# Spectral mixing and a routed mixture of experts: result tiles of 96 rows made into tiles of 128 rows

## The chip, the cores and the metric

The kernel runs on one core of one Trainium2 chip. The metric is the device time of one execution in microseconds. The engines are called as the profile calls them: PE is TensorE (PEld its weight loads), DVE is VectorE, ACT is ScalarE, POOL is GpSimd, SP is SyncE, which here only issues DMAs. A "q" behind a name (SPq, POOLq) is that engine's instruction queue.

## The reference, cut to what matters

```python
# x: (8, 2496, 256) float32; N = 8 * 2496 = 19968 rows; E = 8 experts; F = 1024
X = np.fft.rfft(x, axis=1)
y = np.fft.irfft(X * (filt_r + 1j * filt_i)[None], n=2496, axis=1)     # mixing along the sequence
x = y.reshape(19968, 256)
logits = x @ w_gate + modality_bias[modality_id]                       # 8 logits a row
e_idx = argmax(logits);  gate_w = softmax(logits)[e_idx]
for e in range(8):                                                     # top-1 experts
    mask = e_idx == e
    out[mask] = gate_w[mask, None] * (np.maximum(x[mask] @ w1[e], 0) @ w2[e])
```

## The kernel before, in words

**Transforms.** The length 2496 is split as 48 x 52, and both FFTs are done as small matrix products in three stages per batch. Stage 1 (`stage1`) multiplies 26 tiles of 96 rows by a fixed 96 x 96 matrix and stores the result to DRAM (`b1_d`). Stage 2 (`stage2`) reads it back transposed, multiplies 24 slices of 104 rows, applies the filter and multiplies again, and stores to `b2_d`. Stage 3 (`stage3`) reads `b2_d` back as 26 tiles of 96 rows (`t4`, four DMA loads for tiles 0-7, 8-15, 16-23 and 24-25), multiplies each by the matrix `wbm` (96 x 96, L433) into a PSUM tile `ps`, and evicts two tiles at a time (EV = 2) into `yo`: row `p`, tile `t` is sequence position `26 p + t`. The evictions go to ACT (L451) and DVE (L453) in turn. One step later the two tiles are transposed on PE (L441), copied to SBUF as `yT` (L443), multiplied by the gate weights (L446), and the eight logits of each row are added to `lg` (L456).

**Routing.** When all 26 tiles of a batch are through, `route` finds each row's expert and gate weight and its position in that expert's bin, by DVE operations on tiles of [96, 26, 8] and two small matmuls (L463 to L496). `table` then works out which blocks of 256 rows are full in which bin. `scatter` sends every tile's 96 rows (256 fp16 values, the row number and the gate weight, 520 bytes) to its bin in DRAM with one indirect DMA from POOL (L501), 26 for a batch.

**Experts.** A block is 256 rows of one expert. `load` reads it from its bin (L575, from SP, buffer `xs`, five of them). `turn` copies the expert's w1 (L588), copies row numbers and gate weights out of `xs` into `meta` (L594, three buffers), transposes the rows (L598, L599). `up` (L609) and `down` (L622) run in four quarter steps q of 4 + 4 matmuls of 256 columns, with a ReLU eviction on ACT (L614) between them. After the last quarter DVE multiplies by the gate weights into `osb` (L629, two buffers), and two indirect DMAs from POOL write 128 rows each to the output (L632). These two read `osb` for the data and `meta` for the row numbers, so both buffers are held until the DMA has landed.

**Order.** The main loop below runs 12 iterations `i` of 14 steps `k`. In one iteration stage 1 works on batch i, stage 2 on batch i-1, stage 3 on batch i-2, and the scatters on batch i-3, two of each a step. Each step ends with three quarter steps of the expert work. `route` and `table` for batch i-2 come at the end of an iteration. The number of blocks that are certain to be full by then is fixed (1, 10, 10, 10, 9, 10, 10, and 25 for the last batch, 85 in all), so after the last scatters some 25 blocks remain, which run with nothing beside them. The framework orders the instructions of each engine at build time; on the chip every engine works through its list in that order and waits where it must. A scatter is kept behind the last issued output DMA (`behind("out", 1)`). A block's load waits for all scatters that precede it in the program.

Of the kernel before, what the change touches and what calls it, by code (L numbers as in the profile page):

```python
# [20 lines left out]
P = 128  # L21
# [7 lines left out]
def kernel(  # L29
# [30 lines left out]
    KB = 2 * N2  # L60

# [238 lines left out]
    keep = const_pool.tile([KA, E, NTT], F32)  # L300
# [27 lines left out]

    mid_h = dataclasses.replace(moe_modality_id.tensor, shape=list(moe_modality_id.tensor.shape))
    mid32 = mid_h.ap().bitcast(I32).rearrange("(n two) -> n two", two=2)  # L330
# [18 lines left out]
    NP = NTT // EV  # L349
    st = [dict() for _ in range(B)]  # L350
# [57 lines left out]
    def stage3(g, k):  # L408

        t = k * EV  # L410
        if k == 0:
            yw = yp.tile([KA, NTT, RW], I32, tag="yo", name="yo")
# [3 lines left out]
            nc.sync.dma_start(mid_raw, mid32[g * S:(g + 1) * S].rearrange("(p t) two -> p t two", t=NTT))  # L416
            midf = sp.tile([KA, NTT], F32, tag="midf")
            nc.vector.tensor_copy(midf, mid_raw[:, :, 0])
            lg = sp.tile([KA, NTT, E], F32, tag="lg", bufs=2)
            st[g]["lg"] = lg  # L420
            nc.vector.tensor_mul(lg, midf[:, :, None].to_broadcast([KA, NTT, E]),
                                 biasd[:KA, None, :].to_broadcast([KA, NTT, E]))
            nc.vector.tensor_add(lg, lg, bias0[:KA, None, :].to_broadcast([KA, NTT, E]))
        yo = st[g]["yw"].bitcast(BF16)
        if k < NP:
            c, t0, t1 = chunk_of(t)
            if t == t0:
                src = b2_d[g].rearrange("s (jr t) c -> (s jr) t c", jr=4)
                st[g]["t4"] = bp.tile([KA, TCM, D], BF16, tag="t24", name="t4")
                nc.sync.dma_start(st[g]["t4"][:, 0:t1 - t0, :], src[:, t0:t1, :])  # L430
            ps = pp.tile([P, EV, D], F32, tag="ps")
            for i in range(EV):
                nc.tensor.matmul(ps[:KA, i, :], lhsT=wbm, rhs=st[g]["t4"][:, t - t0 + i, :], start=True, stop=True)  # L433
        if k > 0:
            tb = t - EV
            lt = pp.tile([P, 2 * D], F32, tag="ps")
            pT = lt[:, 0:D].bitcast(BF16).rearrange("p (i a q) -> p i a q", i=EV, a=DC)
            psL = lt[:, D:D + EV * E].rearrange("p (i e) -> p i e", e=E)
            for i in range(EV):
                for dc in range(DC):  # L440
                    nc.tensor.transpose(pT[:, i, dc, :KA], yo[:, tb + i, dc * P:(dc + 1) * P], ident[:KA, :KA])  # L441
            yT = sp.tile([P, EV, DC, KA], BF16, tag="yT", bufs=2)
            nc.vector.tensor_copy(yT, pT[:, :, :, :KA])  # L443
            for i in range(EV):
                for dc in range(DC):
                    nc.tensor.matmul(psL[:KA, i, :], lhsT=yT[:, i, dc, :], rhs=wg[:, dc, :],  # L446
                                     start=(dc == 0), stop=(dc == DC - 1))
        if k < NP:
            dst = yo[:, t:t + EV, 0:D]
            if k % 2:  # L450
                nc.scalar.activation(dst, ps[:KA], AF.Copy, scale=1.0 / S)  # L451
            else:
                nc.vector.tensor_scalar_mul(dst, ps[:KA], 1.0 / S)  # L453
        if k > 0:
            lg = st[g]["lg"]
            nc.vector.tensor_add(lg[:, tb:tb + EV], lg[:, tb:tb + EV], psL[:KA])  # L456

    def route(g):

        yw, lg = st[g]["yw"], st[g]["lg"]  # L460
        b3 = [KA, NTT, E]
        mx = sp.tile([KA, NTT], F32, tag="mx")
        nc.vector.reduce_max(mx, lg, axis=AX.X)  # L463
        oh = sp.tile(b3, F32, tag="oh")
        nc.vector.tensor_tensor(oh, lg, mx[:, :, None].to_broadcast(b3), op=ALU.is_ge)
        nc.vector.tensor_mul(oh, oh, revio[:KA, None, :].to_broadcast(b3))
        wm = sp.tile([KA, NTT], F32, tag="wm")
        nc.vector.reduce_max(wm, oh, axis=AX.X)
        ohT = sp.tile([KA, E, NTT], F32, tag="ohT")
        nc.vector.tensor_tensor(ohT.rearrange("p e t -> p t e"), oh, wm[:, :, None].to_broadcast(b3),  # L470
                                op=ALU.is_equal)
        sc = sp.tile([KA, E, NTT], F32, tag="sc")
        nc.vector.tensor_tensor_scan(sc.rearrange("p e t -> p (e t)"), keep.rearrange("p e t -> p (e t)"),
                                     ohT.rearrange("p e t -> p (e t)"), 0.0, op0=ALU.mult, op1=ALU.add)
        c = sp.tile([KA, E], F32, tag="c")
        nc.vector.tensor_copy(c, sc[:, :, NTT - 1])
        psO = pp.tile([P, 2, E], F32, tag="ps")
        nc.tensor.matmul(psO[:KA, 0, :], lhsT=Lexcl[:KA, :KA], rhs=c, start=True, stop=True)
        nc.tensor.matmul(psO[:, 1, :], lhsT=ones_sq[:KA, :], rhs=c, start=True, stop=True)
        off = sp.tile([KA, E], F32, tag="off")  # L480
        nc.vector.tensor_add(off, cnt[:KA], ecap[:KA])
        nc.vector.tensor_add(off, off, psO[:KA, 0, :])
        nc.vector.tensor_add(cnt, cnt, psO[:, 1, :])
        nc.vector.tensor_add(sc, sc, off[:, :, None].to_broadcast([KA, E, NTT]))
        nc.vector.tensor_mul(sc, sc, ohT)
        pos = sp.tile([KA, NTT], F32, tag="pos")
        nc.vector.reduce_sum(pos, sc.rearrange("p e t -> p t e"), axis=AX.X)
        pos_i = sp.tile([KA, NTT], I32, tag="posi", bufs=2)
# [5 lines left out]
        ssum = sp.tile([KA, NTT], F32, tag="ssum")  # L494
        nc.vector.reduce_sum(ssum, lg, axis=AX.X)
        nc.vector.reciprocal(yw[:, :, DW + 1].bitcast(F32), ssum)  # L496

    def scatter(g, k):
        for t in range(k * EV, (k + 1) * EV):
            with behind("out", 1):  # L500
                ins = nc.gpsimd.indirect_dma_start(  # L501
                    out=bins_d[:, :], out_offset=IOA(ap=st[g]["pos"][:, t:t + 1], axis=0),
                    in_=st[g]["yw"][:, t, :], in_offset=None)
# [76 lines left out]
    def turn(b):  # L580
# [12 lines left out]
        b["meta"] = ep.tile([P, NI, 2], I32, tag="meta", bufs=3, name="meta")  # L593
# [22 lines left out]
    def down(b, q):  # L616
# [8 lines left out]
        if (q + 1) * FQ == FT:  # L625
            osb = ep.tile([P, NI, D], F32, tag="osb", bufs=2)
# [71 lines left out]
    for i in range(B + 4):  # L698
        for k in range(NP + 1):
# [6 lines left out]
            if 0 <= i - 2 < B:  # L706
                stage3(i - 2, k)
            if 0 <= i - 3 < B and k < NP:
# [44 lines left out]
```

## Time and profile before

| | |
|---|---|
| median of 3 runs | 1031.1 us (1027.1 to 1033.96) |
| profiled execution | 1031.97 us, span 1030.2 us (first to last instruction) |
| mean granted TensorE clock | 0.868 |
| PE / DVE / ACT / POOL busy | 662.1 / 424.8 / 387.0 / 409.0 us |
| scatters L501 / output DMAs L632 | 208 / 170 instructions |

The profile is one execution. A row of the groups view gives line, engine and operation, out<-in, count, busy time and mean duration, then the engine's idle time just ahead of these instructions and what ended it. The waits view gives who waited for what: total us, times, longest. The chain view follows the last instruction back through what released it; "another core or an unknown queue", shown as "remote" in the waits, is a release that the profile can't assign. In the timeline the square brackets hold the idle time before and its releaser. The windows view gives busy time of each engine in a stretch of the span. By these, set-up lasts to about 43 us, transforms alone run to about 171 us, scatters begin at 176.9 us and end near 866 us, and the last stretch, from about 870 us, is expert work only.

### The profile page before, as it was taken

Reading aid. Unit: us, or ns where it says so; the run is one execution under the profiler, and the core shown is the slowest. Engines: PE = TensorE matmul, PEld = TensorE weight load, DVE = VectorE, ACT = ScalarE, POOL = GpSimd, SP = SyncE. Lnnn points to the kernel's source line nnn. Section 1 sums busy time; section 2 is a strip of 40 time slices with the busy share of each in tenths; the row PEclk is TensorE's granted clock in tenths of the full one; section 3 lists DMA queues with packets and bytes.
Section 4 is the critical chain, followed back from the end, with each engine's and each line's share of the span. In section 5 each row is a group of like instructions: output and inputs, shape, how many; then the busy total and the mean of one; then the engine's idle time right before and its main releaser. Section 6 shows DMA issues by size and latency. Waiting matters only on the chain.

```text
span 1030.2 us, 16235 instructions
## 1 busy us (share of the span) xinstructions
PE 662.1 (64%) x4966; PEld 526.6 (51%) x4966; DVE 424.8 (41%) x1305; ACT 387.0 (38%) x697; POOL 409.0 (40%) x468
## 2 busy tenths in 40 slices
PE   0316377266645777687677776774777567768776
PEld 0205266255434666566565555563555445656554
DVE  8803145135325344633454463445335322333332
ACT  1115255143433455344444443441333233434333
POOL 6022201712442355435535543544355455333333
PEclk9999999999655898589979986896868787999999
DMA  9299965335436445534553344324111422212210
GB/s 146 36 207 208 219 147 127 91 91 129 108 87 140 115 120 116 129 99 126 123 146 92 96 120 111 91 62 113 58 57 54 118 68 78 73 62 67 68 42 2
DMA packets 95179, 106.66 MB, mean 104 GB/s; under 512 B 13226, under 2 KB 77520, under 8 KB 94994
## 3 DMA queue, kind: packets, MB, share of 16 engines
q0 software_dynamic: 32544, 52.04, 23.0%
q1 hardware_dynamic: 62554, 53.59, 20.1%
q8 instruction: 45, 0.74, 0.3%
q14 instruction: 36, 0.29, 0.1%
HBM read 74.27 MB, written 54.31 MB: 125 GB/s over the span
## 4 chain that ended last, share of the span: by engine, by line
PE 30%; issue 22%; DMA 13%; DVE 12%; another core or an unknown queue 10%; POOL 7%; ACT 4%; DVEq 1%; POOLq 0%; ACTq 0%; SPq 0%
PE hps L609 7%; PE ops L622 7%; DMA t<-b_d 5%; POOL out_dram L632 4%; DMA b_d<-t 4%; POOL bins_d L501 3%; DMA b_d<-z 2%; PE ps L433 2%; PE pz L389 2%; PE lt L446 2%; PE ps L363 2%; PE pz L390 2%; PE ps L382 2%; DVE osb L629 2%
## 5 line engine op out<-in xcount | busy, mean ns | idle before, releaser
L614 ACT ACTIVATE hT<-hps 128x512 f16<-128x512 f32 x340 | 197.0, 597 | 305.0 <-PE hps L609 164.3
L632 POOL DMA_INDIRECT out_dram<-osb,meta x170 | 166.8, 981 | 308.8 <-DVE osb L629 267.2
L622 PE MATMUL ops<-w2sb,hT 128*128 x1360 | 227.6, 291 | 46.8 <-DVE osb L629 46.3
L501 POOL DMA_INDIRECT bins_d<-yo,pos_i x208 | 193.7, 931 | 110.5 <-issue 69.7
L609 PE MATMUL hps<-xT,w 128*128 128x256 f16 x1360 | 222.2, 297 | 23.0 <-ACT hT L614 10.9
L622 PEld LDWEIGHTS <-hT 128*128 128x128 f16 x1360 | 140.6, 105 | 88.6 <-issue 57.7
L609 PEld LDWEIGHTS <-w 128*128 128x128 f16 x1360 | 138.9, 106 | 50.1 <-issue 18.2
L366 ACT CAST t<-ps 96x512 f16<-96x512 f32 x104 | 59.8, 583 | 127.7 <-PE ps L363 73.1
L599 DVE COPY xT<-pT 128x512 f16<-128x512 f16 x85 | 36.0, 424 | 146.4 <-PE pT L598 83.3
L403 ACT CAST z<-pz 104x512 f16<-104x512 f32 x96 | 56.7, 590 | 84.5 <-remote 30.7
L130 POOL DMA_DIRECT2D xt<-in_x_dram x32 | 18.2, 570 | 169.6 <-PE ps L363 158.8
L396 DVE TENSOR_TENSOR p<-xf,g 104x512 f16<-104x512 f16 x96 | 40.3, 420 | 109.1 <-ACT xf L394 94.4
L382 PE MATMUL ps<-t,w2m 104*104 104x256 f16 x192 | 52.8, 369 | 49.3 <-DMA t<-b_d 40.5
L389 PE MATMUL pz<-p,a1m 104*104 104x256 f16 x192 | 68.1, 364 | 21.0 <-issue 6.6
L433 PE MATMUL ps<-t,wbm 96*96 96x256 f16 x208 | 56.1, 354 | 37.4 <-DMA t<-b_d 15.2
L629 DVE TENSOR_SCALAR osb<-ops,meta 128x256 f32<-128x256 f32 x170 | 74.3, 476 | 9.3 <-PE ops L622 5.5
L363 PE MATMUL ps<-xt,w1m 96*96 96x256 f16 x208 | 59.0, 380 | 24.4 <-ACT z L403 8.5
L394 ACT CAST xf<-ps 104x512 f16<-104x512 f32 x96 | 56.3, 588 | 48.1 <-PE ps L382 34.2
L446 PEld LDWEIGHTS <-yT 128*96 128x96 f16 x416 | 40.9, 162 | 63.0 <-DVE yT L443 43.7
L446 PE MATMUL lt<-wg,yT 128*96 128x8 f16 x416 | 41.8, 207 | 47.2 <-DVE yT L443 32.7
L588 DVE COPY w<-w1sb 128x2048 f16 x85 | 58.8, 692 | 23.7 <-PE hps L609 18.1
L390 PE MATMUL pz<-xf,a2m 104*104 104x256 f16 x192 | 68.2, 365 | 0.0
(179 smaller groups left out, 687.3 us busy)
## 6 DMA issues: line engine op xcount, KB each, us to landing
xs<-bins_d SPq DMA_DIRECT2D x85, 130.0 KB
t<-b_d SPq DMA_DIRECT2D x24, 416.0 KB
b_d<-z SPq DMA_DIRECT2D x48, 208.0 KB
xt<-in_x_dram POOLq DMA_DIRECT2D x24, 384.0 KB
b_d<-t SPq DMA_DIRECT2D x48, 192.0 KB
t<-b_d SPq DMA_DIRECT2D x24, 384.0 KB
w1sb<-in_moe_w_dram POOLq DMA_DIRECT2D x8, 512.0 KB
w2sb<-in_moe_w_dram POOLq DMA_DIRECT2D x8, 512.0 KB
```

Of the source, the lines that this page charges most:

```text
L363: nc.tensor.matmul(ps[:KA, i, :], lhsT=w1m, rhs=xt[:, t - t0 + i, :], start=True, stop=True)
L382: nc.tensor.matmul(ps[:KB, i, :], lhsT=w2m[:, s + i, :], rhs=st[g]["t2"][:, s % SCH + i, :], start=True, stop=True)
L389: nc.tensor.matmul(pz[:KB, i, :], lhsT=a1m[:, s_ + i, :], rhs=p1[:, i, :], start=True, stop=False)
L390: nc.tensor.matmul(pz[:KB, i, :], lhsT=a2m[:, s_ + i, :], rhs=p2[:, i, :], start=False, stop=True)
L433: nc.tensor.matmul(ps[:KA, i, :], lhsT=wbm, rhs=st[g]["t4"][:, t - t0 + i, :], start=True, stop=True)
L446: nc.tensor.matmul(psL[:KA, i, :], lhsT=yT[:, i, dc, :], rhs=wg[:, dc, :], start=(dc == 0), stop=(dc == DC - 1))
L501: ins = nc.gpsimd.indirect_dma_start(out=bins_d[:, :], out_offset=IOA(ap=st[g]["pos"][:, t:t + 1], axis=0), in_=st[g]["yw"][:, t, :], in_o ...
L609: mm = nc.tensor.matmul(hps[:, k, :], lhsT=b["w1"][:, dc, ft * P:(ft + 1) * P], rhs=b["xT"][:, dc].rearrange("p i t -> p (i t)"), start=(d ...
L614: nc.scalar.activation(b["hT"][:, q * FQ:(q + 1) * FQ, :], hps, AF.Relu)
L622: nc.tensor.matmul(b["ops"][:, i, :], lhsT=b["hT"][:, ft, i * P:(i + 1) * P], rhs=w2sb[:, ds(b["ej"], 1), ft, :], start=(ft == 0 and i == ...
L629: nc.vector.tensor_scalar_mul(osb[:, i, :], b["ops"][:, i, :], gate[:, i, :])
L632: ins = nc.gpsimd.indirect_dma_start(out=out[:, :], out_offset=IOA(ap=b["meta"][:, i, 0:1], axis=0), in_=osb[:, i, :], in_offset=None, **kw)
```

## The change

PSUM and SBUF have 128 partitions; stage 3 used 96. The 26 tiles of a batch become 20: of every four tiles (0-3, 4-7, ..., 20-23) three stay, and the fourth one's 96 rows are computed in three pieces of 32 rows into partitions 96 to 127 of the other three, by a second matmul with 32 columns of `wbm`. Tiles 24 and 25 stay at 96 rows, and their partitions 96 to 127 hold copies that are masked out. So `yo`, `lg` and everything in `route` are [128, 20, ...]; stage 3 ends at step 10 of an iteration, not 13, and there are 20 scatters a batch (18 of 128 rows, 2 of 96). Row numbers come from a table `tok` made once; POOL adds the batch's offset to it. The modality numbers of all batches are loaded and rearranged once in the set-up (`mids`), by four DMAs and seven small DVE copies, instead of per batch. The `t4` loads are issued at steps 0, 3, 6 and 9 (before: 0, 4, 8, 12). Beside this, `meta` gets 8 buffers instead of 3 and `osb` 3 instead of 2.

```diff
+    KC = P - KA                       # 32
+    NYF = NTT // 4 * 3                # 18
+    NY = NYF + 2                      # 20
+    NYG = NTT // 4                    # 6
...
+    tok = const_pool.tile([P, NY, 1], I32)          # three iotas on POOL
...
+    mids = const_pool.tile([P, B, NY], BF16)
+        mraw = mp.tile([P, B, 2 * NTT], I32)
+        nc.sync.dma_start(mraw[:KA], mid32)
+        for b in range(3):
+            nc.vector.tensor_copy(mids[:KA, :, b:NYF:3], mv[:KA, :, b:4 * NYG:4, 0])
+        nc.vector.tensor_copy(mids[:KA, :, NYF:NY], mv[:KA, :, 4 * NYG:NTT, 0])
+        nc.vector.memset(mids[KA:P, :, NYF:NY], 0.0)
+        for b in range(3):
+            nc.sync.dma_start(mraw[KA:P], mid32[b * KC:(b + 1) * KC])
+            nc.vector.tensor_copy(mids[KA:P, :, b:NYF:3], mv[KA:P, :, 3:4 * NYG:4, 0])
...
+    NPY = NY // EV                    # 10
...
-            nc.gpsimd.iota(yw[:, :, DW:DW + 1], pattern=[[1, NTT], [1, 1]], base=g * S, channel_multiplier=NTT)
-            mid_raw = sp.tile([KA, NTT, 2], I32, tag="midr")
-            nc.sync.dma_start(mid_raw, ...)
-            nc.vector.tensor_copy(midf, mid_raw[:, :, 0])
+            nc.gpsimd.tensor_single_scalar(yw[:, :, DW:DW + 1], tok, g * S, op=ALU.add)
...
-            if t == t0:
+            if k % 3 == 0:
                 ... load of t4 ...
             for i in range(EV):
-                nc.tensor.matmul(ps[:KA, i, :], lhsT=wbm, rhs=st[g]["t4"][:, t - t0 + i, :], start=True, stop=True)
+                nc.tensor.matmul(ps[:KA, i, :], lhsT=wbm, rhs=t4[:, t - t0, :], start=True, stop=True)
+                nc.tensor.matmul(ps[KA:P, i, :], lhsT=wbm[:, c0:c0 + KC], rhs=t4[:, tc_ - t0, :],
+                                 start=True, stop=True)
...
-                    nc.tensor.transpose(pT[:, i, dc, :KA], yo[:, tb + i, dc * P:(dc + 1) * P], ident[:KA, :KA])
+                    nc.tensor.transpose(pT[:, i, dc, :], yo[:, ub + i, dc * P:(dc + 1) * P], ident)
...  (route: [KA, NTT, E] becomes [P, NY, E] throughout)
+        nc.vector.memset(ohT[KA:P, :, NYF:NY], 0.0)
...
     def scatter(g, k):
+            rows = P if t < NYF else KA
-                    out=bins_d[:, :], out_offset=IOA(ap=st[g]["pos"][:, t:t + 1], axis=0),
+                    out=bins_d[:, :], out_offset=IOA(ap=st[g]["pos"][:rows, t:t + 1], axis=0),
...
-        b["meta"] = ep.tile([P, NI, 2], I32, tag="meta", bufs=3, name="meta")
+        b["meta"] = ep.tile([P, NI, 2], I32, tag="meta", bufs=8, name="meta")
...
-            osb = ep.tile([P, NI, D], F32, tag="osb", bufs=2)
+            osb = ep.tile([P, NI, D], F32, tag="osb", bufs=3)
...
-            if 0 <= i - 2 < B:
+            if 0 <= i - 2 < B and k <= NPY:
                 stage3(i - 2, k)
-            if 0 <= i - 3 < B and k < NP:
+            if 0 <= i - 3 < B and k < NPY:
                 scatter(i - 3, k)
```

More of the change, by code (lines that the diff above doesn't have):

```diff
@@ L60 @@
     KB = 2 * N2
+    KC = P - KA
+    assert KA == 3 * KC and NTT % 4 == 2
+    NYF = NTT // 4 * 3
+    NY = NYF + 2
+    NYG = NTT // 4
     BLK = 256
@@ L477, in route @@
+        nc.vector.tensor_copy(c, sc[:, :, NY - 1])
         psO = pp.tile([P, 2, E], F32, tag="ps")
[L478 to L482, printed above, removed]
+        nc.tensor.matmul(psO[:, 0, :], lhsT=Lexcl, rhs=c, start=True, stop=True)
@@ L483, in route @@
+        nc.tensor.matmul(psO[:, 1, :], lhsT=ones_sq, rhs=c, start=True, stop=True)
+        off = sp.tile([P, E], F32, tag="off")
+        nc.vector.tensor_add(off, cnt, ecap)
+        nc.vector.tensor_add(off, off, psO[:, 0, :])
         nc.vector.tensor_add(cnt, cnt, psO[:, 1, :])
-        nc.vector.tensor_add(sc, sc, off[:, :, None].to_broadcast([KA, E, NTT]))
+        nc.vector.tensor_add(sc, sc, off[:, :, None].to_broadcast([P, E, NY]))
         nc.vector.tensor_mul(sc, sc, ohT)
-        pos = sp.tile([KA, NTT], F32, tag="pos")
+        pos = sp.tile([P, NY], F32, tag="pos")
@@ L487, in route @@
         nc.vector.reduce_sum(pos, sc.rearrange("p e t -> p t e"), axis=AX.X)
[L488 removed]
+        pos_i = sp.tile([P, NY], I32, tag="posi", bufs=2)
         nc.vector.tensor_copy(pos_i, pos)
```

70 lines of the change are left out of this document (39 added, 31 removed).

## The prediction

> **What bounds the kernel now.** I read the page's span, busy times and the chain of work that ended last; then the windows, to see where one bound gives way to the next; then the waits and the timeline of the stretches in which the change acts.
>
> ```profile
> span 1030.2 us, 16235 instructions
> ...
> PE 662.1 (64%) x4966; PEld 526.6 (51%) x4966; DVE 424.8 (41%) x1305; ACT 387.0 (38%) x697; POOL 409.0 (40%) x468
> ...
> by line: issue 22.5%; another core or an unknown queue 9.6%; PE hps L609 7.4%; PE ops L622 6.7%; DMA t<-b_d 4.9%; POOL out_dram L632 4.4%; DMA b_d<-t 4.1%; POOL bins_d L501 3.0%; DMA b_d<-z 2.5%; PE ps L433 2.3%; PE pz L389 2.1%; PE lt L446
> ```
>
> The profiled execution took 1031.97 us, of which 1.8 lie around the span; the sum below is made against it. It stands 0.9 above the median of 1031.1 us. No engine is full over the span: PE has 64%, POOL 40%. So the kernel is bound by who waits for whom, and two entries of the chain matter for this change. One is the 9.6% that the profile can't assign ("another core or an unknown queue", 99 us of the span). The other is the output DMA, L632, with the waits hung on it. The windows show two regimes.
>
> ```profile
> core 0: us, PE busy (x) PEld busy (x) DVE busy (x) ACT busy (x) POOL busy (x), PEclk, DMA share, GB/s
> ...
> 517.00:613.00 96.00, 72.43 (x602) 59.02 (x601) 46.15 (x150) 45.29 (x84) 43.54 (x47) 0.88 0.41 113
> ...
> 870.00:1026.00 156.00, 119.76 (x946) 90.28 (x944) 52.57 (x130) 59.39 (x104) 54.56 (x56) 0.94 0.18 57
> ```
>
> In a middle iteration (517 to 613) PE is busy 72.43 of 96 us; in the last stretch, expert work alone, 119.76 of 156, at a clock of 0.94. Both leave PE idle for about a quarter of the time. What ends the idle time differs.
>
> **The last stretch: meta and osb.** The first two rows are waits in 870 to 1026, the rest is the timeline.
>
> ```profile
> DVE meta L594 <- DMA out_dram<-osb,meta: 41.8, 25, 4.0
> ...
> PE ops L622 <- DVE osb L629: 23.4, 23, 2.8
> ...
> 869.57 0.87 DVE L629 TENSOR_SCALAR osb<-ops,meta 128x256 f32<-128x256 f32 x2
> ...
> 964.69 0.60 PE L622 MATMUL ops<-w2sb,hT 128*128 x4
> ...
> 965.19 0.17 DVE L594 COPY meta<-xs 128x4 int32<-128x4 int32 x1 [1.18 <-DMA out_dram<-osb,meta]
> ...
> 965.92 0.87 DVE L629 TENSOR_SCALAR osb<-ops,meta 128x256 f32<-128x256 f32 x2
> 966.68 0.98 POOL L632 DMA_INDIRECT out_dram<-osb,meta  x1 [3.12 <-DVE osb L629]
> ...
> 966.85 1.21 PE L622 MATMUL ops<-w2sb,hT 128*128 x8 [0.68 <-DVE osb L629]
> 967.97 0.98 POOL L632 DMA_INDIRECT out_dram<-osb,meta  x1 [0.30 <-issue]
> ...
> 970.58 0.17 DVE L594 COPY meta<-xs 128x4 int32<-128x4 int32 x1 [1.23 <-DMA out_dram<-osb,meta]
> ...
> 1011.15 0.87 DVE L629 TENSOR_SCALAR osb<-ops,meta 128x256 f32<-128x256 f32 x2
> ```
>
> Follow one block. L594 copies `meta` at 965.19 only after an output DMA has landed; `osb` (L629) stands behind it on DVE and starts at 965.92. POOL issues the two output DMAs at 966.68 and 967.97, the second is issued at 968.95, and 1.63 us later `meta` of the next block may start, at 970.58. This is a closed ring of 5.39 us: osb, two DMA issues, landing, meta, osb. PE is not the bound in it: its last `ops` matmuls start at 964.69 and end at 965.29, so `osb` is 0.63 us late. From 869.57 to 1011.15 there are 25 such waits, 5.66 us a block.
>
> With eight `meta` buffers the wait is for an output DMA eight blocks back, long landed; `osb` then waits for the DMA three blocks back instead of two, looser too. The ring opens. Next late is PE with its single `ops` bank: 5.39 - 0.63 + 0.1 for the signal = 4.85 us, an estimate from these rows. **25 x (5.66 - 4.85) = 20 us gained.** Bounds: if the cycles with slow landings stay long, 25 x 0.53 = 13; if all of PE's wait for osb goes, 23.
>
> **The same wait in the middle.**
>
> ```profile
> DVE meta L594 <- DMA out_dram<-osb,meta: 89.8, 55, 4.0
> ...
> by line: issue 17.0%; PE hps L609 12.3%; PE ops L622 11.0%; another core or an unknown queue 9.3%; DMA out_dram<-osb,meta 5.0%; DVE osb L629 3.9%; PE lt L446 3.1%; DVE w L588 3.0%; PE pT L598 2.8%; DVE p L396 2.5%; DVE yT L443 2.4%; PE pz L
> ```
>
> Of 89.8 us in all, 41.8 lie in the last stretch, 48.0 before. There DVE also carries evictions and products of the transforms, queued behind `meta`, and PE waits for those. But the chain passes through "DMA out_dram" for only 5.0% of 92 us, 4.6 us, in the iteration from 613 to 705; over five iterations at most 23. The stage after it (PE, ACT) is often late as well. **I take 8**, between 0 and 23.
>
> **Fewer scatters.**
>
> ```profile
> L501 POOL DMA_INDIRECT bins_d<-yo,pos_i x208 | 193.7, 931 | 110.5 <-issue 69.7 <-DVE incl L527 26.4 <-DVE off L481 13.0
> L632 POOL DMA_INDIRECT out_dram<-osb,meta x170 | 166.8, 981 | 308.8 <-DVE osb L629 267.2 <-issue 32.0 <-DVE yT L443 2.3
> ...
> 195.78 0.39 PEld L446 LDWEIGHTS <-yT 128*96 128x96 f16 x4 [2.44 <-issue]
> 196.12 0.92 POOL L501 DMA_INDIRECT bins_d<-yo,pos_i  x1 [0.30 <-issue]
> ...
> 205.92 0.92 POOL L501 DMA_INDIRECT bins_d<-yo,pos_i  x1 [0.31 <-issue]
> ...
> 210.81 0.17 DVE L456 TENSOR_TENSOR lg<-lg,lt 96x16 f32<-96x16 f32 x1 [14.75 <-remote]
> ...
> by line: issue 59.6%; POOL bins_d L501 29.5%; POOL out_dram L632 11.8%; POOLq L632 0.2%
> ...
> by line: issue 67.3%; POOL out_dram L632 21.4%; PE ops L622 3.4%; DMA out_dram<-osb,meta 1.5%; PE hps L609 1.4%; DVE osb L629 1.0%; POOLq L632 0.9%; POOLq L748 0.8%; DVE w L588 0.8%; PE pT L598 0.7%; DVEq L586 0.4%; DVE xT L599 0.3%; DVE me
> ```
>
> The cost of one indirect DMA on POOL hardly depends on its rows: 931 ns with 96 rows, 981 with 128 rows of twice the bytes. So 208 scatters become 160, each at 0.93 to 0.98: 37 to 45 us less of POOL. POOL's own busy time is not the path in most of the span. Two things make it count.
>
> First, signals from PE. Four logit matmuls start at 195.78, and DVE's add, which needs only them, starts at 210.81 after 14.75 us "remote", while POOL issues one scatter after the other (196.12 to 205.92). The chain of 870 to 1030, with no scatters, lists no unassigned time. So a run of scatters holds back what PE has finished, and this is most of the 99 us. If it goes with their number, 48/208 of it leaves: 23 us. Ends: 0, if it goes with rows or bytes, which stay; 99, if the 128-row form does as little harm as the output DMAs, which have 128 rows. The nearest row is L501 itself, so I start from 23, and since the next releaser on each such path is not far, **I take 15**.
>
> Second, in 800 to 870 the chain is POOL: 29.5% of 70 us is 20.7 us for 26 scatters. Six fewer are 4.8 us: **5**, between 0 and 8 with the gaps between them.
>
> Scatters also end at step 9. POOL's addition into `yw`, in place of the iota, waits for the DMAs of an older batch, and loads of blocks wait for the scatters ahead of them; both wait for work that is now older. What stands behind that addition on POOL is the next batch's scatters and outputs.
>
> **Stage 3 on PE, DVE and ACT.**
>
> ```profile
> L433 PE MATMUL ps<-t,wbm 96*96 96x256 f16 x208 | 56.1, 354 | 37.4 <-DMA t<-b_d 15.2 <-DVE lg L456 13.9 <-issue 4.3
> ...
> L441 PE MATMUL lt<-ident,yo 96*128 96x96 f16 x416 | 45.6, 244 | 24.5 <-ACT t L366 15.3 <-issue 4.8 <-DVE yo L453 2.3
> ...
> L453 DVE TENSOR_SCALAR yo<-ps 96x512 f16<-96x512 f32 x56 | 38.3, 683 | 43.7 <-PE ps L433 33.3 <-PE hps L609 5.0 <-remote 2.7
> ...
> L443 DVE COPY yT<-lt 128x384 f16<-128x384 f16 x104 | 36.5, 351 | 50.3 <-remote 32.1 <-PE hps L609 6.3 <-PE lt L441 6.1
> L599 DVE COPY xT<-pT 128x512 f16<-128x512 f16 x85 | 36.0, 424 | 146.4 <-PE pT L598 83.3 <-issue 25.9 <-remote 17.6
> ...
> L465 DVE TENSOR_TENSOR oh<-lg,mx 96x208 f32<-96x208 f32 x8 | 3.0, 371 | 0.3
> ```
>
> PE: a batch has 26 + 52 + 52 matmuls, transposes and logit matmuls before, 40 + 40 + 40 after. The 354 ns are a pipelined instruction's length; in a stream, from the `ops` rows above, (1.21 - 0.60)/4 = 0.15 us each. Fourteen more of 256 columns cost 2.1 us, 24 fewer small ones give back about half: 1 us a batch, 8 in all at full clock, half of it on the path, **4 lost**. Below nothing: 8 gained, if the 32-column matmul runs beside its neighbour. The upper end is the rival below. The eviction of `ps` now waits for four matmuls instead of two; behind it on ACT and DVE stand the experts' ReLU and `osb`.
>
> The Trainium skill, page "TensorEngine Tiling (Array Packing)", section "Key Properties", says that changing the tiling mode drains the TensorE, and that tiles work independently. A matmul of 32 columns into partitions 96 to 127 would be such a change of mode, twice for each; the rows here hold no such matmul and can't tell. By the first half of that rule the rival below comes out, by the second the gain of 8 above.
>
> DVE: two evictions fewer (2 x 0.683), 13 x 0.351 for `yT` becomes 10 x 0.424 by the equally large `xT` copy, and about eleven operations of `route` shrink from 26 to 20 columns (0.371 to 0.29): some 3 us a batch, 24 in all. DVE's work is mostly beside PE's; **3** of the 24 on the path, between 0 and 24.
>
> **The seam between iterations.** `route` and `table` follow the last logits, and the next blocks' loads follow them. Stage 3 now ends three steps earlier, so this chain can run under steps 11 to 13.
>
> ```profile
> 531.00:600.00 69.00, 52.92 (x471) 43.30 (x469) 28.95 (x83) 34.16 (x63) 33.13 (x35) 0.93 0.38 107
> 600.00:631.00 31.00, 18.31 (x127) 13.11 (x124) 16.77 (x67) 9.56 (x18) 15.58 (x17) 0.70 0.43 117
> ```
>
> PE is busy 18.31 of 31 us in the seam and 52.92 of 69 beside it: 59% against 77%, 5.5 us lost at a seam, 28 at five. Whether the order fixed at build time pulls `route` forward can't be seen from before. **I take 8**, between 0 and 28.
>
> **DMAs that move, and the set-up.**
>
> ```profile
> PE ps L433 <- DMA t<-b_d: 15.2, 7, 3.4
> ...
> L418 DVE CAST midf<-mid_raw 96x26 f32<-96x26 int32 x8 | 2.6, 327 | 0.9 <-DMA mid_raw<-in_moe_modality_id_dram 0.9
> ```
>
> The `t4` loads sit on SP's queue behind the stores of steps 3, 6 and 9 instead of 4, 8 and 12. With the three buffers that `t24` shares with stage 2, before, loads at steps 4 and 8 needed a buffer just used; after, only stage 2's at step 4 does. PE waited 15.2 us for `t4` in all: **3 gained**, between 0 and 15. In the set-up come three reloads of `mraw`, each behind the copy before it: in the open 3 x (1.63 landing + 0.33), and seven copies at 0.33 on DVE, 8 us at worst; SP idles then and the copies fit into DVE's early gaps in part: **3 lost**, between 0 and 8. Later, eight copies L418 are gone.
>
> **The sum.** 20 + 8 + 15 + 5 + 3 + 8 + 3 gained = 62; 4 + 3 lost = 7; 55 us net. 1031.97 - 55 = **977 us**. The terms' own bounds, not all at one end, make 953 to 1000.
>
> **Rivals.**
>
> *The middle doesn't follow.* Its stalls are many and small; with one releaser gone the next is as late. Then only the last stretch (20) and 800 to 870 (5) count, less 7: 1014 us. For it: the middle's PE waits have no one cause. Against: unassigned time is one cause, and large.
>
> *The scatters are fewer but not cheaper*, so that the change doesn't do what it says: with POOL's time going by rows, 128/96 x 0.931 = 1.24 us, 160 make 199 us against 193.7. The terms 15 and 5 vanish: 997 us. Against: 981 ns at 128 rows.
>
> *The held-back signals go with the 96-row form, and the seam closes.* 55 instead of 15 and 20 instead of 8: 977 - 52 = 925 us. For it: the last stretch, with 128-row DMAs only, has no unassigned time. Against: there the DMAs come in pairs, not in runs.
>
> *Slower: PE pays for the 32-column matmuls.* There are 160, each between two matmuls of another shape; if the array empties before and after each, the price falls on PE, in order, where three quarter steps of expert work queue behind it. It decides from (55 + 4)/160 = 0.37 us each on the path; at 0.5 us, 80 us replace the 4: 1053 us. For it: no row shows such a matmul. Against: a matmul lasts 0.35 us from start to end here (L433), so emptying the array around it should cost about as much beyond its stream time, and PE is idle a quarter of the time.
>
> **How the numbers follow.** Chances: forecast 0.58, middle doesn't follow 0.13, scatters not cheaper 0.09, large gain 0.13, slower 0.07. The range takes in the forecast's own bounds and the two smaller gains, and part of the large one: 935 to 1018; it leaves out the slower case and the lower half of the large gain. About 1%, 10 us, is what a measurement of this kernel can tell from no change. Faster by over 1%: the forecast, both scatter cases and the greater part of the case of 1014: 0.87; within 1%: the rest of that case and mishaps of a few of the terms together, 0.07; slower 0.06.
>
> **What the profile after would show.** In the last stretch: no wait of `meta` for out_dram, `osb` directly after `ops`, 4.7 to 5.0 us a block. L501: 160 instructions of under 1 us. The unassigned share of the chain: below 9.6%, near 8. L433: 320 matmuls, with the idle time just ahead of the 32-column ones the mark of the slower rival. The scan of `route` soon after step 10, the next batch's first scatter earlier in the iteration. The forecast is wrong if L594 still waits or another buffer takes its place (`xs`, `osb`), if L433's idle time grows by tens of us, or if stage 1 starts well after 43 us.

## The result: 949 us, and the profile after

| | before | after |
|---|---|---|
| median, both run on one chip | 1029.1 us (1023.73 to 1033.96, 4 runs) | 949.34 us (944.64 to 954.9, 4 runs) |
| ratio | | 0.9228, 95% interval 0.9148 to 0.9308 |
| profiled execution, span | 1031.97, 1030.2 us | 945.37, 943.6 us |
| granted clock | 0.868 | 0.827 |

The change takes 80 us off, more than the 55 of the forecast. Ratios leave out executions in a slower state; of the kernels below only the control has one, 868.96 us, and without it the control's median is 857.66. The page after, then the line of its chain:

```profile
span 943.6 us, 15937 instructions
...
PE 656.2 (70%) x4886; PEld 488.5 (52%) x4886; DVE 408.8 (43%) x1249; ACT 382.0 (40%) x689; POOL 376.1 (40%) x423
...
PEclk9997555555565799869989998999789699999999
...
by line: PE hps L642 12.6%; PE ops L655 11.9%; issue 10.9%; DMA b_d<-t 6.9%; another core or an unknown queue 5.9%; DMA t<-b_d 5.5%; PE ps L463 3.7%; PE ps L462 3.5%; DMA b_d<-z 3.4%; PE lt L472 3.1%; PE pT L631 2.8%; PE ps L411 2.6%; DVE o
```

PE has nearly the work that it had and fills more of a shorter span. Releases that the profile can't assign fall from 9.6% to 5.9% of the chain. In the waits view all rows "remote" together fall from 213.9 us to 112.9. The first row below is before's, the one that the prediction's argument rests on; the other three are after's, and the second of them is the same wait:

```profile
DVE lg L456 <- remote: 56.2, 8, 14.7
...
ACT hT L647 <- remote: 38.1, 10, 7.3
...
DVE lg L487 <- remote: 6.6, 2, 5.0
...
ACT xf L423 <- remote: 1.0, 2, 0.8
```

The last stretch: two rows of its waits (807 to 926), then the timeline of a block. Lines have moved: `meta` is L627, `osb` L662, the output DMA L665, the copy of `w` L621.

```profile
DVE meta L627 <- DMA out_dram<-osb,meta: 0.3, 1, 0.3
...
PE ops L655 <- DVE osb L662: 6.7, 23, 1.0
...
855.93 0.69 DVE L621 COPY w<-w1sb 128x2048 f16 x1 [0.89 <-PE hps L642]
...
856.54 0.87 DVE L662 TENSOR_SCALAR osb<-ops,meta 128x256 f32<-128x256 f32 x2
...
857.33 0.17 DVE L627 COPY meta<-xs 128x4 int32<-128x4 int32 x1
857.46 1.17 PE L655 MATMUL ops<-w2sb,hT 128*128 x8 [0.26 <-DVE osb L662]
...
861.56 0.87 DVE L662 TENSOR_SCALAR osb<-ops,meta 128x256 f32<-128x256 f32 x2
```

`meta` waits for no output, PE waits 0.26 us for `osb` instead of 0.68, and the next block's `osb` comes after 5.02 us; over 16 blocks the mean period is 4.94 us. The windows of a middle iteration and of the last stretch, and the two kinds of indirect DMA:

```profile
478.00:565.00 87.00, 68.12 (x565) 52.18 (x564) 42.13 (x134) 42.73 (x80) 39.72 (x42) 0.90 0.45 124
807.00:930.00 123.00, 105.43 (x902) 81.86 (x901) 49.92 (x121) 56.94 (x100) 49.09 (x50) 1.00 0.22 68
...
L665 POOL DMA_INDIRECT out_dram<-osb,meta x170 | 167.1, 983 | 294.5 <-DVE osb L662 250.5
L534 POOL DMA_INDIRECT bins_d<-yo,pos_i x160 | 157.0, 981 | 66.5 <-issue 52.7
```

PE is now busy 78% of a middle iteration (75% before) and 86% of the last stretch (77%). Where the 86.6 us between the two spans went, by four marks (the first matmul of stage 1 of the fourth batch, the 53rd, 61st and 85th copy of `w`):

| | before | after | gained |
|---|---|---|---|
| start to fourth batch | 171.2 | 172.8 | -1.6 |
| to block 53: batches with scatters | 641.2 | 582.1 | 59.1 |
| to block 61: last scatters | 56.6 | 52.0 | 4.6 |
| to block 85: experts alone | 141.5 | 118.2 | 23.3 |
| to the end | 19.7 | 18.5 | 1.2 |

### The profile page after: what moved, and what is told of

It is laid out like the page before. It is cut to its first block, busy times and chain, and to the rows that moved or that the text cites. A ratio compares the mean times of both kernels' runs of the same rounds, so it can differ in the third digit from the quotient of the medians.

```text
span 943.6 us, 15937 instructions
## 1 busy us (share of the span) xinstructions
PE 656.2 (70%) x4886; PEld 488.5 (52%) x4886; DVE 408.8 (43%) x1249; ACT 382.0 (40%) x689; POOL 376.1 (40%) x423
## 4 chain that ended last, share of the span: by engine, by line
PE 48%; DMA 17%; issue 11%; DVE 11%; another core or an unknown queue 6%; ACT 4%; POOL 2%; DVEq 1%; SPq 0%; POOLq 0%; ACTq 0%
PE hps L642 13%; PE ops L655 12%; DMA b_d<-t 7%; DMA t<-b_d 6%; PE ps L463 4%; PE ps L462 3%; DMA b_d<-z 3%; PE lt L472 3%; PE pT L631 3%; PE ps L411 3%; DVE osb L662 2%; PE ps L392 2%; PE pz L418 2%; PE pz L419 2%
## 5 line engine op out<-in xcount | busy, mean ns | idle before, releaser
L665 POOL DMA_INDIRECT out_dram<-osb,meta x170 | 167.1, 983 | 294.5 <-DVE osb L662 250.5
L642 PE MATMUL hps<-xT,w 128*128 128x256 f16 x1360 | 216.3, 293 | 26.8 <-ACT hT L647 22.9
L655 PE MATMUL ops<-w2sb,hT 128*128 x1360 | 216.0, 281 | 21.7 <-DVE osb L662 20.8
L534 POOL DMA_INDIRECT bins_d<-yo,pos_i x160 | 157.0, 981 | 66.5 <-issue 52.7
L642 PEld LDWEIGHTS <-w 128*128 128x128 f16 x1360 | 137.2, 105 | 56.4 <-DVE xT L632 17.7
L655 PEld LDWEIGHTS <-hT 128*128 128x128 f16 x1360 | 135.7, 101 | 58.9 <-issue 31.2
L411 PE MATMUL ps<-t,w2m 104*104 104x256 f16 x192 | 50.3, 352 | 82.2 <-DMA t<-b_d 71.9
L621 DVE COPY w<-w1sb 128x2048 f16 x85 | 58.9, 693 | 66.5 <-PE hps L642 51.3
L662 DVE TENSOR_SCALAR osb<-ops,meta 128x256 f32<-128x256 f32 x170 | 74.4, 476 | 9.0 <-PE ops L655 6.3
L411 PEld LDWEIGHTS <-w2m 104*104 104x104 f16 x192 | 30.0, 166 | 83.8 <-DMA t<-b_d 66.5
L462 PE MATMUL ps<-t,wbm 96*96 96x256 f16 x160 | 55.9, 349 | 18.5 <-DMA t<-b_d 10.4
L418 PE MATMUL pz<-p,a1m 104*104 104x256 f16 x192 | 63.7, 344 | 5.0 <-DVE p L425 2.5
L419 PE MATMUL pz<-xf,a2m 104*104 104x256 f16 x192 | 63.1, 341 | 0.9 <-DVE xf L426 0.9
L392 PE MATMUL ps<-xt,w1m 96*96 96x256 f16 x208 | 55.2, 362 | 11.1 <-ACT t L395 5.4
L631 PE MATMUL pT<-ident,xs 128*128 128x128 f16 x340 | 36.5, 232 | 34.8 <-issue 23.8
```

Source lines behind the costliest of these rows:

```text
L392: nc.tensor.matmul(ps[:KA, i, :], lhsT=w1m, rhs=xt[:, t - t0 + i, :], start=True, stop=True)
L411: nc.tensor.matmul(ps[:KB, i, :], lhsT=w2m[:, s + i, :], rhs=st[g]["t2"][:, s % SCH + i, :], start=True, stop=True)
L418: nc.tensor.matmul(pz[:KB, i, :], lhsT=a1m[:, s_ + i, :], rhs=p1[:, i, :], start=True, stop=False)
L419: nc.tensor.matmul(pz[:KB, i, :], lhsT=a2m[:, s_ + i, :], rhs=p2[:, i, :], start=False, stop=True)
L462: nc.tensor.matmul(ps[:KA, i, :], lhsT=wbm, rhs=t4[:, t - t0, :], start=True, stop=True)
L534: ins = nc.gpsimd.indirect_dma_start(out=bins_d[:, :], out_offset=IOA(ap=st[g]["pos"][:rows, t:t + 1], axis=0), in_=st[g]["yw"][:rows, t, ...
```

## The experiments

They ran in three sets, each on another chip, always beside the kernel before. On the first and third chip it took 1029 and 1027 us; on the second 902. That difference became an experiment of its own. Where this part says that a kernel reached a block, it means that block's copy of `w`, as in the table above. "Control" is the changed kernel run again on the second chip.

**The meta ring alone (first chip).** The kernel before with

```
-        b["meta"] = ep.tile([P, NI, 2], I32, tag="meta", bufs=3, name="meta")
+        b["meta"] = ep.tile([P, NI, 2], I32, tag="meta", bufs=6, name="meta")
```

> The kernel before with six meta buffers instead of three and nothing else (eight, or a third osb, do not fit into SBUF beside the larger routing tiles of before). Theory (the sum of the prediction): the ring of output DMA, meta and osb opens in the last stretch, 24 blocks from 5.9 to about 4.95 us, 23 us, and some 8 us in the middle: about 998 us, 0.97 of before. Rival A, the middle has other waits as late: only the last stretch, 1006 us, 0.978. Rival B, the meta wait is most of the whole change, since DVE waited 48 us for it in the middle as well: 965 us or less, 0.94.

Measured: 1030.76 us, ratio 1.0011 (0.9982 to 1.0041): nothing. The waits view of its last stretch and a piece of its timeline:

```profile
DVE meta L594 <- DMA out_dram<-osb,meta: 33.7, 21, 3.4
...
880.55 0.87 DVE L629 TENSOR_SCALAR osb<-ops,meta 128x256 f32<-128x256 f32 x2
881.33 0.41 DVE L599 COPY xT<-pT 128x512 f16<-128x512 f16 x1
881.66 0.16 DVE L594 COPY meta<-xs 128x4 int32<-128x4 int32 x1
885.18 0.17 DVE L594 COPY meta<-xs 128x4 int32<-128x4 int32 x1 [3.35 <-DMA out_dram<-osb,meta]
```

Counting rows from the start of the trace, the copy at 885.18 is the 65th, and the `osb` at 880.55 belongs to block 59: with six buffers copy 65 needs the buffer of block 59, whose outputs have just been issued. In the profile before, with three buffers, copy 63 needs the buffer of block 60, whose `osb` stood just ahead of it too. The copies have moved ahead in VectorE's order by as much as the buffers were added, so the ring is as tight as it was.

**The 128-row tiles alone (first chip).** The changed kernel with `meta` 3 and `osb` 2.

> The changed kernel with three meta and two osb buffers, as before: the 128-row tiles alone. Theory: about 949 + 31 = 980 us, 0.952 of before; last stretch back at 5.4 to 5.9 us a block with L-meta waiting for out_dram; the unassigned share of the chain as low as in the changed kernel (about 6%). Rival B (the buffers are most of it): 1000 us or more, 0.975. Rival C (the two parts need each other, the sum of both alone is less than both together): e1 and e2 together gain clearly less than 80 us.

Measured: 964.96 us, ratio 0.9372 (0.9336 to 0.9408), 64 us below before and 15 below the 980 of the theory. In its last stretch (811 to 946) the old wait is back:

```profile
DVE meta L627 <- DMA out_dram<-osb,meta: 38.0, 24, 3.8
```

From block 61 to block 85 it takes 135.0 us, against 118.2 with the ring open: 16.8, and the whole kernel differs by 964.96 - 949.34 = 15.6. So the medians leave next to nothing for the ring outside the last stretch, though the two intervals are too wide to exclude some us. The rows carry four fifths of the gain.

**Which buffers (second chip).** The changed kernel with `osb` at 2 and with `meta` at 6.

```
-            osb = ep.tile([P, NI, D], F32, tag="osb", bufs=3)
+            osb = ep.tile([P, NI, D], F32, tag="osb", bufs=2)
```

> The changed kernel with 2 osb buffers and not 3; meta stays at 8. Theory A (the 8 meta buffers alone opened the ring, since each row of osb waits for an output two blocks back, about 9.9 us, and that one has landed): within 4 us of the control, block period in the last stretch 4.9 to 5.0 us. Rival B (both rings had to open): 10 to 20 us above the control, osb rows waiting for outputs, period 5.3 to 5.4 us.

> The changed kernel with 6 meta buffers and not 8; osb stays at 3. Theory A (the meta copies are put into VectorE's order as early as their buffers allow, up to the five xs buffers: in the trace of before with 6 of them the 65th copy stands after the 59th block's osb, and its buffer is freed by that very block's output, as with 3 of them, where the 63rd stands after the 60th; in the changed kernel with 8 the 81st stands after the 73rd but one cycle behind its output): the wait for an output is back in the last stretch, 1.3 to 1.8 us a block over some 25 blocks, period 5.3 to 5.4 us, 10 to 18 us above the control. Rival B (6 are enough once osb has 3): within 4 us of the control, no such wait.

> The changed kernel once more, unaltered, as the control for the three kernels beside it. Every theory: 945 to 955 us, ratio 0.918 to 0.928.

Measured: control 860.64 us, ratio 0.9525 (0.9472 to 0.9578), which misses its expectation (below, 857.66 stands for it); `osb` 2: 858.79, 0.9512 (0.946 to 0.9565); `meta` 6: 867.52, 0.9596 (0.9539 to 0.9653). The waits of `meta` in the last stretch, first with `osb` 2, then with `meta` 6:

```profile
DVE meta L627 <- DMA out_dram<-osb,meta: 0.3, 1, 0.3
```

```profile
DVE meta L627 <- DMA out_dram<-osb,meta: 39.3, 23, 3.8
```

The third `osb` buffer does nothing; eight `meta` buffers open the ring and six don't, as theory A of both has it. With eight, copy 80 follows the `osb` of block 73 in the first trace of after and needs block 72's buffer, an output one cycle older. The price with six is 19 us in the last stretch (137.2 against 117.8 from block 61 to 85, `osb` 2) but 10 over the kernel, at the lower end of theory A: it reached block 61 at 710.5 us, 10.6 ahead of the one with `osb` 2. Why is open.

**More scatters (first chip).** The changed kernel with 144 scatters more, of 32 rows each, from `yw` into a tensor that nothing reads:

```
+            if t < NYF:
...
+                ins = nc.gpsimd.indirect_dma_start(
+                    out=trash_d[:, :], out_offset=IOA(ap=tri[:KC, n:n + 1], axis=0),
+                    in_=st[g]["yw"][:KC, t, :], in_offset=None)
```

> The changed kernel with 144 more scatters: after each scatter of 128 rows, one of 32 rows of the same tile into a DRAM tensor that nobody reads. Rows sent rise by 23%, indirect DMAs of this line from 160 to 304. Theory (a scatter holds back PE's signals by its number): remote waits and the unassigned part of the chain nearly double, from 56 to about 100 us, and the time rises by 25 to 45 us to 975 to 995. Rival (they go with rows or bytes): remote waits rise by a quarter at most, unassigned about 69 us, time within 15 us of 949 as far as POOL, with some 130 us more work, is not itself late.

Measured: 1111.97 us, ratio 1.0828 (1.0787 to 1.0869): 163 us above the changed kernel, 1.13 us for each. That is far outside both the theory (25 to 45 us) and the rival (15). Groups and waits:

```profile
L547 POOL DMA_INDIRECT trash_d<-yo,tri x144 | 127.5, 885 | 54.9 <-issue 49.0
...
ACT hT L659 <- remote: 67.1, 14, 13.6
DVE lg L490 <- remote: 52.8, 7, 11.2
```

A scatter with a quarter of the rows takes POOL 885 ns, nearly as long as a full one (981), so its price goes by number and hardly by rows. All "remote" rows together rise from 112.9 to 285.3 us, and POOL's busy time from 376.1 to 503.1. So the 1.13 us may be late signals, POOL's own 0.89 us for each, or both. If the 48 scatters that the change saves cost as much each, they would be 54 of the rows' 64 us, an estimate.

**Signals held back, or a clock? (second and third chip).** From the semaphore events of each trace one can take, for every matmul that signals, the time from its start to the next move of PE's semaphore. For matmuls that start within 1 us of a scatter's record and of no output DMA, it is 1.02 us on average before (280 matmuls), 0.90 after (198) and 1.64 with the 144 scatters more (309); with neither scatter nor output near, 0.25 to 0.27. (Some moves are missing from the traces, so these are rough.) On the second chip it is 0.25 us beside scatters too (control, 260 matmuls), and no "remote" row is left. The page of the kernel with `osb` 2 there:

```profile
span 857.7 us, 15947 instructions
...
PE 632.7 (74%) x4886; PEld 473.9 (55%) x4886; DVE 409.9 (48%) x1249; ACT 382.9 (45%) x689; POOL 381.5 (44%) x423
...
PEclk9999555555578699889999999997989899999999
```

POOL needs as long as on the first chip for as many instructions (381.5 against 376.1 us), and the changed kernel still takes 92 us less. To have the kernel before in the same light, and the price of a scatter:

> The kernel before, unaltered, for its trace: its times were near 1029 us in the first runs and near 902 us in the second ones, on another chip. Theory A (the 127 us are TensorE's signals that came late beside the scatters on the first chip and not on the second): with a time near 902, a matmul beside a scatter tells the others within 0.25 to 0.45 us of its start (0.9 to 1.0 us on average in the first trace), granted clock within 0.03 of the first trace's 0.868; with a time near 1029, the first trace again. Rival B (the second chip grants TensorE a higher clock): with a time near 902 a clock above 0.93 and the signals as late as before.

> The changed kernel with 144 more scatters of 32 rows again; on the first chip they cost 163 us, 1.13 us each. Theory A (what they cost is that they hold back TensorE's signals): where before takes about 902 us and signals are not held back, 0 to 45 us above the changed kernel (0 to 0.3 us each, for GpSimd's order alone), ratio 0.95 to 1.00; where before takes about 1029 us, 150 to 175 us again, ratio 1.07 to 1.09. Rival B (their price is GpSimd's own second for each, and GpSimd's order is on the path): 130 to 165 us on either chip, ratio 1.09 to 1.14 where before takes 902 us.

Both fell to the third chip, which behaves as the first: 1029.72 us, and 1111.01, ratio 1.0818 (1.0747 to 1.089), with signals of the kernel before at 1.11 us beside scatters. So neither run told its theory A and rival B apart: the price of a scatter where nothing is held back wasn't measured, and the kernel before has no trace on the second chip. The clock as the cause of the 127 us is out, though. The stretch from the third batch's start to the fifth's, before on the first chip and again on the third:

```profile
107.00:245.00 138.00, 76.43 (x469) 66.03 (x468) 50.44 (x170) 50.92 (x92) 33.35 (x41) 1.00 0.61 131
```

```profile
107.00:248.00 141.00, 75.68 (x468) 65.51 (x468) 50.15 (x169) 50.71 (x92) 33.24 (x41) 0.51 0.61 131
```

Half the granted clock costs 3 us in 138 here. Nor was the second chip's clock much higher: the kernel before had 0.82 to 0.87 there, beside the second set, and 0.79 to 0.84 beside the first.

**Stage 3 three steps later (first chip).** What the seam is worth: stage 3 ends at step 13 again, as before, with tiles of 128 rows.

```
-            if 0 <= i - 2 < B and k <= NPY:
-                stage3(i - 2, k)
+            if 0 <= i - 2 < B and 0 <= k - 3 <= NPY:
+                stage3(i - 2, k - 3)
```

> The changed kernel with stage 3 shifted by three steps, so that it ends at step 13 of an iteration as before; scatters, rows and buffers unchanged. Theory (the early end of stage 3 lets routing, table and the first loads run under steps 11 to 13): the seam opens again, 2 to 6 us an iteration in seven iterations, 960 to 985 us. Rival (the seam is hidden anyway, what the middle gained are the scatters): within 5 us of 949.

Measured: 944.07 us, ratio 0.9198 (0.9152 to 0.9244), no slower than the changed kernel. The theory's 960 to 985 us is out. But the marks show that this hides two differences. The fourth batch starts 12.1 us earlier than in the changed kernel's trace (160.7 against 172.8), and from there to block 61 it takes 9.9 us more (644.0 against 634.1). The stretch from about 107 us up to the fourth batch, in the changed kernel and in this one:

```profile
107.00:172.00 65.00, 42.43 (x223) 28.70 (x221) 19.85 (x59) 25.69 (x47) 5.98 (x9) 0.50 0.73 145
```

```profile
107.00:161.00 54.00, 31.39 (x232) 21.65 (x230) 20.88 (x62) 25.69 (x48) 6.72 (x10) 0.98 0.94 193
```

The granted clock was 0.50 in one and 0.98 in the other, and PE is busy 65% and 58% of the stretch. So the gain there may be the clock or the later stage 3, and the 9.9 us, where the seams lie, may be the seam. One pair of traces can't tell: the two kernels with `meta` 6 and `osb` 2 differ by as much (8.6 us) from the fourth batch to block 61, without any change to stage 3. What the seam is worth stays open.

**The 32-column matmuls (second, then third chip).** First the order: both 96-column matmuls of a pair of tiles, then both 32-column ones.

```
                 nc.tensor.matmul(ps[:KA, i, :], lhsT=wbm, ...)
+            for i in range(EV):
                 nc.tensor.matmul(ps[KA:P, i, :], lhsT=wbm[:, c0:c0 + KC], ...)
```

> The changed kernel with the matmuls of stage 3 in another order: the 96-column ones of the two tiles of a group first, then the 32-column ones, so that the shape changes 162 times and not 320. Theory A (a change of shape takes TensorE about 0.1 us, from starts 0.21 us apart where shapes alternate against 0.11 us apart for equal ones, and it lies on the path): 158 changes fewer are 16 us of TensorE, of which half or more shows: 8 to 16 us below the control. Rival B (the price is paid beside other work, TensorE waits there for the t4 loads and the evictions anyway): within 4 us of the control. Rival C (the second 96-column matmul now waits for the second load before the first tile's 32 columns are done): 3 to 6 us above.

Then no change of shape at all: two matmuls of 128 columns, padded with zeros, add up in PSUM.

```
-                nc.tensor.matmul(ps[:KA, i, :], lhsT=wbm, rhs=t4[:, t - t0, :], start=True, stop=True)
-                nc.tensor.matmul(ps[KA:P, i, :], lhsT=wbm[:, c0:c0 + KC], ..., start=True, stop=True)
+                nc.tensor.matmul(ps[:, i, :], lhsT=wbz, rhs=t4[:, t - t0, :], start=True, stop=False)
+                nc.tensor.matmul(ps[:, i, :], lhsT=wby[:, c0 // KC, :], ..., start=False, stop=True)
```

> The changed kernel with stage 3 written without narrow matmuls: the 96-column matrix is filled up with 32 columns of zeros, the 32-column one with 96 columns of zeros ahead, and both matmuls of a tile add up in the same 128 rows of PSUM, so that the shape never changes; as many matmuls as the changed kernel. Theory A (a change of shape takes 0.09 us, and 320 of them are on TensorE's path, as 158 fewer gave 15 us on the second chip): 22 to 30 us below the changed kernel, that is ratio 0.92 to 0.93 where before takes 902 us and 0.895 to 0.905 where it takes 1029 us; stage-3 matmuls start 0.11 us apart. Rival B (what the grouped order gained was not the change of shape but the place of the second 96-column matmul): within 5 us of the changed kernel (ratio 0.947 to 0.958, or 0.918 to 0.928).

Measured: 845.42 us in the grouped order, ratio 0.9384 (0.934 to 0.9428) against the control's 0.9525, 12.2 us less; padded 922.7 us, ratio 0.8974 (0.8931 to 0.9017), 26.6 below the changed kernel's 949.34 on a chip where before takes as long. PE's group of the 32-column matmuls in the changed kernel and its timeline around a pair of tiles, then the timeline in grouped order, and padded:

```profile
L463 PE MATMUL ps<-t,wbm 96*32 96x256 f16 x160 | 52.9, 330 | 0.0
...
493.76 0.27 PE L419 MATMUL pz<-xf,a2m 104*104 104x256 f16 x1
493.97 0.27 PE L462 MATMUL ps<-t,wbm 96*96 96x256 f16 x1
494.17 0.28 PE L463 MATMUL ps<-t,wbm 96*32 96x256 f16 x1
494.38 0.31 PE L462 MATMUL ps<-t,wbm 96*96 96x256 f16 x1
494.62 0.28 PE L463 MATMUL ps<-t,wbm 96*32 96x256 f16 x1
494.83 0.40 PE L472 MATMUL lt<-ident,yo 128*128 128x128 f16 x4
```

```profile
457.82 0.38 PE L462 MATMUL ps<-t,wbm 96*96 96x256 f16 x2
458.14 0.39 PE L466 MATMUL ps<-t,wbm 96*32 96x256 f16 x2
458.46 0.40 PE L475 MATMUL lt<-ident,yo 128*128 128x128 f16 x4
```

```profile
471.83 0.27 PE L469 MATMUL ps<-t,wbz 96*128 96x256 f16 x1
471.95 0.27 PE L470 MATMUL ps<-t,wby 96*128 96x256 f16 x1
472.06 0.27 PE L469 MATMUL ps<-t,wbz 96*128 96x256 f16 x1
472.16 0.27 PE L470 MATMUL ps<-t,wby 96*128 96x256 f16 x1
472.27 0.39 PE L479 MATMUL lt<-ident,yo 128*128 128x128 f16 x4
```

From the first of the four matmuls to the transposes: 0.86, 0.64 and 0.44 us. The price is not that of any change of shape. Over the traces of these three kernels, where the granted clock is 1.00, matmuls of 256 columns with stationary matrices of 96, 104 or 128 columns mostly start 0.11 us apart, equal shapes or not, and two of 32 columns in a row 0.12 (grouped). Only a change to or from 32 columns takes 0.20 to 0.24. So such a change costs TensorE about 0.1 us, and 320 of them some 30. The rule in the Trainium skill, "TensorEngine Tiling (Array Packing)", "Key Properties", that a change of tiling mode drains the TensorE, agrees; the page gives no price.

That all of the 26.6 us is this price is argued, not shown. The padded kernel's order of instructions differs on VectorE and ScalarE too, which the framework chose anew; the grouped one, beside its own matmuls, only has a few others of TensorE elsewhere. And of the 18.3 us between the two traces, 10.9 lie before the fourth batch's start (161.9 us against 172.8), where only an eighth of the changes lie and the granted clock from 107 us on was 0.66 against 0.50. At 0.50 a change costs 0.11 to 0.17 us (starts 0.33 to 0.38 us apart against 0.21). The grouped order halves the changes and gains 12.2, which agrees with about 25 for all of them.

**One step further (third chip).** The padded kernel with 3 `w1` and 2 `osb` buffers.

> The same with 3 w1 buffers and 2 osb buffers: the copies of w need not wait for the up matmuls of two blocks back (0.9 us of VectorE's waiting a block in the last stretch). Theory A (the next up matmuls wait for that copy): 3 to 8 us below the kernel with the filled-up matrices, block period under 4.85 us in the last stretch. Rival B (TensorE is the bound there, the copy is early enough): within 3 us of it, period 4.9 to 5.0 us.

Measured: 921.45 us, ratio 0.8971 (0.8923 to 0.9019), the same as padded alone, period 4.93 us. Rival B's time holds: the copy of `w` is early enough. The padded kernel beats both kernels, by 10% and by 26.6 us.

## Why the prediction was right, and which of its terms were not

The direction, the last stretch and the price by number were read rightly. That 977 came within 28 us of 949 is in part luck: the scatters gave more than was forecast, stage 3 took more, and the two errors stood against each other.

- **Last stretch, 20 gained.** Right in size and place: 23.3 between the traces, 16.8 with the rows held equal. Its working was loose. From 869.57 to 1011.15 there are 25 `osb` but 24 intervals, 5.90 us each and not 5.66; and the ring opens not because there are more buffers than three but because eight exceed what the copies run ahead, which six don't. A third `osb` buffer had no part in it.
- **The same wait in the middle, 8.** Not seen: the last stretch's 16.8 us cover the whole 15.6 between the medians. From the fourth batch to block 61 the kernel with the ring closed took 6.4 us more in one pair of traces (`meta` 3 against 8) and 8.6 less in another (`meta` 6 against `osb` 2), so no effect of 8 stands out. That the next releaser is as late, as the chain of before had hinted, would explain it.
- **Held-back signals, 15.** The term that was most undersized, if signals are what the scatters cost. The price goes by number, as argued, but the 23 us came from the unassigned share of one chain, and the discount to 15 from nothing measured. By the first chip's 1.13 us, 48 scatters are 54 us, POOL's own time included. By the second chip, where the changed kernel's signals aren't late, the whole change is worth 902 - 858 = 44 us against 80, of which rows about 34 (44 less the 10 by which `meta` 6 is above the control) against 64: the late signals would be some 30. Between 30 and 54, then, as an estimate. What failed here is reading a cost from the share of one chain: 144 scatters more cost 163 us, where that reading gave 25 to 45.
- **POOL in 800 to 870, 5.** 4.6 gained there (block 53 to 61, 52.0 us). The traces of four kernels with as many scatters, on the first and third chip, gave 50.8 to 55.2, so the close match is partly luck.
- **Stage 3 on PE, 4 lost.** Too small: some 25 lost, by the 12.2 us for half of the changes and the 26.6 for all. The rival that was to make it slower had the place right, a price before and after each narrow matmul, at up to 0.17 us of path for each of 160, below the 0.37 from which it would have decided. The sign that was to show it, PE's idle time just ahead of these matmuls, is 0.0 us: the price shows in the distance of the starts, since a matmul's record (330 ns) is longer than that. The gain on the scatters hid the error.
- **DVE, 3.** DVE's busy time fell by 16.0 us, not 24 (the rows that it was added up from give 2.6 us a batch, 21 in all); what of it was on the path wasn't tried alone.
- **The seam, 8.** Open: the kernel with stage 3 three steps later is no slower in all, but its trace took 9.9 us more from the fourth batch to block 61 and 12.1 less ahead of it, at another granted clock.
- **Loads of t4, 3, and set-up, 3 lost.** PE's wait for `t4` ahead of stage 3's first matmul fell from 15.2 to 10.4 us; stage 1 starts at 43.5 us in both traces, so the set-up costs nothing.
- **What stays open.** Rows are worth about 34 us on the second chip, with some 25 lost to narrow matmuls, so about 60 us would come from other than late signals: fewer POOL instructions, transposes, evictions. No run divided these.

Of the rivals, the scatters are cheaper by number, so 997 falls; the case of 925 had much of its first half, the scatters; its second, the seam, wasn't shown.

## What to carry to other kernels

Count indirect DMAs, not their rows: one of 32 rows took POOL 0.89 us and one of 128 rows 0.98, and on the first chip each of the former cost 1.13 us of the kernel's time. When you fill spare partitions with a matmul of 32 columns, pad its matrix with zeros to the full width and let PSUM add, since TensorE paid about 0.1 us for each change to and from 32 columns here. A ring of buffers is open only when it is longer than the distance by which the order of instructions lets its first writer run ahead.

## What the hardware showed that I had not expected

- The same two kernels took 1029 and 949 us on one chip, 902 and 858 on another. The changed kernel's traces differ in how late PE's signals come beside scatters (0.90 us against 0.25), not in how long POOL takes for one (0.98 against 1.00). What in the chip makes it so no run shows.
- In the kernel before, PE's granted clock from the third batch's start to the fifth's was 1.00 in one execution and 0.51 in another, for 138 and 141 us: there that stretch isn't bound by PE.
- A change between matmuls of 96 or more stationary columns and of 32 cost about 0.1 us, nearly the 0.11 us at which a matmul of 256 moving columns follows another; a change between 96, 104 and 128 cost nothing like it.
